# Small steps of a tuned attention-and-SoLU kernel move from VectorE to ScalarE and GpSimd

## The chip, the cores and the metric

The kernel runs on one NeuronCore of a Trainium2 chip. The metric is the device time of one execution in microseconds (us), as the median of several runs. The core's engines run side by side, each through its own list of instructions in order: TensorE (PE, with its weight loads as PEld), VectorE (DVE), ScalarE (ACT), GpSimd (POOL), and SyncE (SP), which issues the DMA transfers. An instruction that waits for another engine holds everything behind it on its own.

## The reference

Set attention with 32 inducing points, then a feed-forward block with the SoLU activation and a layer norm. There are 4 batches of 12608 rows of 128.

```python
def mab(q, kv):
    s = scale * (q @ kv.transpose(0, 2, 1))
    s = s - s.max(-1, keepdims=True)
    a = np.exp(s)
    a /= a.sum(-1, keepdims=True) + 1e-09
    return a @ kv
h = mab(I, x)            # x: (4, 12608, 128), I: (4, 32, 128)
x = mab(x, h)            # then reshaped to (50432, 128)
...
h = x @ w_in             # (50432, 1024)
e = np.exp(h - np.max(h, axis=-1, keepdims=True))
solu = h * (e / (np.sum(e, axis=-1, keepdims=True) + 1e-09))
mu = np.mean(solu, axis=-1, keepdims=True)
var = np.mean((solu - mu) ** 2, axis=-1, keepdims=True)
ln = (solu - mu) / np.sqrt(var + 1e-06) * g_ln
return ln @ w_out        # (50432, 128)
```

## The kernel before

Rows are worked in tiles of 128, 99 tiles a batch (the last one is half full), 396 in all. Tiles of the feed-forward part go in groups of four, and five groups (20 tiles) share one *finish*. There are 20 finishes.

The stages:

- **First pass of a batch** (`p1`): blocks of 12 or 16 tiles are loaded, transposed, scored against the inducing points, and pooled with a running maximum. Batch 0's runs at the start by itself; the first passes of batches 1 to 3 run beside the main work of the batch ahead of them. `P1_STEP` sets how many tiles apart their blocks start.
- **Attention of a block of 16 tiles** (`p2`): scores, transposition (line 840) and maximum (842) on DVE, subtraction on POOL (845), exponential on ACT (852), transposes on PE (875) and copies on ACT (889). The row sums `nr` are reduced on DVE (908), negated with 1e-9 added (911), and inverted to `rn` (914). The negated norm is there so that the next stage's minimum is the negative of a maximum.
- **Main work, tile by tile** (`main`, `soft`): a matmul with the attention's result folded into `w_in` (PE, 1013) leaves 128x1024 in PSUM (`h`). DVE scales it by `rn` into `hn` and takes the minimum `nm` (1054, "the norm"). ACT takes the exponential into `e` with its sum (1065). POOL multiplies `hn` by `e` (1069, "the product"). ACT squares that for the sum of squares (1080), and DVE transposes it in 32x32 blocks into `vt` (1093). The sums go through DRAM to their places (`floor`, 1110 and 1118, by DMA).
- **Second matmul** (`products`, 1136, PE) by `w_out`, with a column of ones that gives each row's total, in two streams. A copy out of PSUM (`evacuate`, 1159) runs on DVE or ACT, whichever the planner has free first.
- **Finish** (`finish`, 1185 to 1198, then 1205): for 20 tiles at once, on 128x20 numbers. Variance from the sum of squares and the total, a floor `z` from the sum of exponentials, the inverse root through `Ln` and `Exp` on ACT, and one Newton step. Then POOL scales the five groups' results by `y` (1205) and SP stores them (1217).

In the program's names, `eu` and `spare` are buffers of 128x1024 that hold `e` or `hn`; `fin` is the finish's small tiles; `dl` is the sums as they come back from DRAM; `qe` is where ACT leaves them.

The order on each engine is made when the program is built. A planner (`Planner.run`) keeps a clock for each engine, a cost for every operation (the second argument of `Op`), and delays between engines; among the operations that could start soon it takes the one with the lowest priority number. The constants `PR_*` are added to the tile's number `t` to make that priority: `PR_MU` the product, `PR_SQ` the square, `PR_TU` the transposition, `PR_G2` the second matmul. `finish` asks for its operations one after the other, each with the operations that it has to wait for; each of DVE's small ones is entered at a cost of 75 ns.

Buffers are handed out by locks. Of the four tiles of `spare` that are free after the start, `HN_MORE` go to the lock for `hn` (which has three others) and the rest to the one for `e` (which has five).

Of the kernel before, what the change touches and what calls it, by code (L numbers as in the profile page):

```python
# [13 lines left out]
AF = mybir.ActivationFunctionType  # L14
ALU = mybir.AluOpType
# [7 lines left out]
FF = 1024  # L23
# [29 lines left out]
EUS = 5  # L53
SPARES = 9
H_LAST = -30
HN_MORE = 3
RAWS = 2
FILL = 400
FIRST = 4
LATE = -15  # L60
P1_FROM = 3
P1_GO = -20
P1_STEP = 11
P2_AHEAD = 35
P2_START = 35
PR_EX = -2
PR_EV = -20
PR_FI = 40
PR_G2 = 4
PR_HN = -4  # L70
PR_MU = 1
PR_SQ = 1
PR_TU = 4
RUSH = -100.0
SLACK = {"PE": 0, "ACT": 200, "DVE": 100, "POOL": 100, "SP": 0}
SPARE = 150
# [53 lines left out]
class Planner:  # L130
# [8 lines left out]
    def spawn(self, gen, prio):  # L139
        self._step([gen, prio, 0], None)  # L140
# [8 lines left out]
    def give(self, lock, buf, *after):  # L149
        lock.free.append((buf, after))  # L150
        while lock.free and lock.waiting:
            lock.waiting.sort(key=lambda w: (w[2], w[1]))
            task = lock.waiting.pop(0)[0]
            self.blocked -= 1
            self._step(task, lock.free.pop(0))
# [95 lines left out]
def set_attention_then_solu_kernel(ctx: ExitStack, tc: tile.TileContext, x, inducing, w_in, w_out, g_ln, out):  # L251
    nc = tc.nc
    NB, N, _ = x.shape
    scale = 1.0 / float(C) ** 0.5
# [26 lines left out]
    def buf(shape, name, dtype=F32, where=None):  # L281
        return (where or const).tile(shape, dtype, name=name)
# [7 lines left out]
    def small(i, **widths):  # L290
# [42 lines left out]
    tiny = buf([P, 1], "tiny")  # L333
# [6 lines left out]
        out=fold[:, 0, :], in_=ident.rearrange("p (q m) -> p m q", m=M), op=ALU.add, axis=AX.X  # L340
    )
    for q in range(1, 4):
# [4 lines left out]
        out=quarter, in_=ident.rearrange("p (q m) -> p q m", m=M), op=ALU.add, axis=AX.X  # L347
# [45 lines left out]
    def dma(nbytes, fn, *after, prio=None, issue=450):  # L393
        return Op("SP", issue + DMA_GAP, fn, *after, prio=prio, moves=nbytes)
# [411 lines left out]
    def p2(b, j):  # L806
        s0, n = at_groups[b][j]
# [3 lines left out]
        for k, (g0, gn) in enumerate(p1_groups[b]):  # L811
            if g0 < s0 + n and s0 < g0 + gn:
                d = yield xd_done[(b, k)]
                prev += d
        xT, rel = yield X2
        d = yield dma(
            n * P * C * 4,
            lambda: nc.sync.dma_start(xT[:, :n, :].rearrange("p s t -> p (s t)"), xT_dram[b][:, s0 * P : (s0 + n) * P]),
            rel, prev,
        )  # L820
# [8 lines left out]
        def scores():  # L829
            for g in range(4):  # L830
# [7 lines left out]
        d = yield Op("PE", SWITCH + n * 60, scores, d, rel, hd)  # L838
        give(X2, xT, d)
        d = yield Op("DVE", 66 + 33.4 * n, lambda: nc.vector.transpose(out=s2[:, :n, :].rearrange("p s m -> p (s m)"), in_=sp[:, : n * M]), d, srel)  # L840
        give(bank, sp, d)
        d = yield Op("DVE", 66 + 33.4 * n, lambda: nc.vector.tensor_reduce(out=mx[:, :n], in_=s2[:, :n, :], op=ALU.max, axis=AX.X), d)  # L842
        d = yield Op(
            "POOL", 60 + 61.4 * n,
            lambda: nc.gpsimd.tensor_tensor(  # L845
                out=s2[:, :n, :], in0=s2[:, :n, :], in1=mx[:, :n].unsqueeze(2).to_broadcast([P, n, M]), op=ALU.subtract
            ),
            d,
        )
        a4, arel = yield A4  # L850
        twice = s2[:, :n, None, :].to_broadcast([P, n, 2, M])
        de = yield Op("ACT", 90 + 54 * n, lambda: nc.scalar.activation(a4[:, :n], twice, AF.Exp, scale=scale), d, arel)
# [53 lines left out]
        for _ in range(2):  # L906
            spawn(turned_rows(), PRIO_P2(b, j))
        d = yield Op("DVE", 66 + 33.4 * n, lambda: nc.vector.tensor_reduce(out=nr[:, :n], in_=a4[:, :n, 0, :], op=ALU.add, axis=AX.X), de)
        d = yield Op(
            "DVE", 75,  # L910
            lambda: nc.vector.tensor_scalar(out=nr[:, :n], in0=nr[:, :n], scalar1=-1.0, scalar2=-1e-9, op0=ALU.mult, op1=ALU.add),  # L911
            d,
        )
        dr = yield Op("DVE", 138, lambda: nc.vector.reciprocal(rn[:, :n], nr[:, :n]), d, rel)
        give(S2, (s2, mx, nr), dr)
        plan.set(turned_too, dr)
# [55 lines left out]
    def PRIO_P1(b, k):  # L972
        return -20.0 + k if b == 0 else NT * (b - 1) + P1_FROM + P1_STEP * k + P1_GO

# [70 lines left out]
    def soft(t, b, j, s, hp, d):  # L1045
# [22 lines left out]
        give(NM, nm, de)  # L1068
        d = yield Op("POOL", 2330, lambda: nc.gpsimd.tensor_tensor(out=e, in0=hn, in1=e, op=ALU.mult), de, prio=t + PR_MU)  # L1069
        give(HN, hn, d)  # L1070
# [7 lines left out]
        def square():  # L1078
            ds = yield Op(
                "ACT", 1040, lambda: nc.scalar.activation(sq, e, AF.Square, scale=1.0 / 32.0, accum_out=G["qe"][:, s, 0:1]), d,  # L1080
                prio=t + PR_SQ,
            )
# [13 lines left out]
            ),  # L1096
            d, rel, prio=t + PR_TU,
        )
# [24 lines left out]
    def products(b, j, t, w):  # L1123
# [21 lines left out]
        ready = max(d.end + AFTER[d.eng]["PE"] for a in (G["turned"], rel, wc_ready.after) for d in a if d is not None)  # L1145
        stream[w].update(j=0, emit=emit, ready=ready, close=close, prio=t + PR_G2)
        idle = flow["idle"]
# [3 lines left out]
    def evacuate(b, j, w, op, bank, dop, prio):  # L1151

        F = fin[(b, j // FG)]
        rows = ff_groups[j][1] * M
        i0 = j % FG * 4 + 2 * w
        rel = yield F["buf"]

        def copied(eng):
            return lambda: eng(F["raw"][:rows, i0 : i0 + 2, :], op[:rows, :, : C + 1])  # L1159

        d = yield Op("DVE", 340, copied(nc.vector.tensor_copy), dop, rel, prio=prio, alt=Op("ACT", 265, copied(nc.scalar.copy), dop, rel, prio=prio))
        give(H, bank, d)
        F["out"].append(d)
        F["left"] -= 1
        if not F["left"]:
            spawn(finish(b, j // FG), prio + PR_FI)

    def finish(b, f):
        F = fin[(b, f)]
        js = [j for j in range(NG) if j // FG == f]  # L1170
        rows = ff_groups[js[0]][1] * M
        w = 4 * len(js)
        fd = []
        for j in js:
            d = yield grp[(b, j)]["floor"]
            fd += d
        part, v, y, root, z = (F[k][:rows, :w] for k in ("part", "v", "y", "root", "z"))
        Q, S = (F["dl"][:rows, :w, i] for i in range(2))
        tt, ts, stt = nc.vector.tensor_tensor, nc.vector.tensor_scalar, nc.vector.scalar_tensor_tensor
        total = F["raw"][:rows, :w, C]  # L1180

        def small(fn, *after):
            return Op("DVE", 75, fn, *after)

        de = yield small(lambda: ts(out=z, in0=S, scalar1=1e-3, scalar2=1e-12, op0=ALU.mult, op1=ALU.add), fd)  # L1185
        de = yield small(lambda: tt(out=z, in0=z, in1=z, op=ALU.mult), de)  # L1186
        d = yield small(lambda: stt(out=part, in0=total, scalar=1.0 / (FF * FF), in1=total, op0=ALU.mult, op1=ALU.mult), F["out"])  # L1187
        d = yield small(lambda: tt(out=v, in0=Q, in1=part, op=ALU.subtract), fd, d)
        d = yield small(lambda: stt(out=v, in0=v, scalar=0.0, in1=z, op0=ALU.max, op1=ALU.add), d, de)

        def inverse():
            nc.scalar.activation(y, v, AF.Ln)
            nc.scalar.activation(root, y, AF.Exp, scale=-0.5)

        da = yield Op("ACT", 330, inverse, d)
        d = yield small(lambda: stt(out=z, in0=root, scalar=-0.5, in1=root, op0=ALU.mult, op1=ALU.mult), da)
        d = yield small(lambda: tt(out=z, in0=z, in1=v, op=ALU.mult), d)  # L1197
        dy = yield small(lambda: stt(out=y, in0=z, scalar=1.5, in1=root, op0=ALU.add, op1=ALU.mult), d, da)
        used = []
        for j in js:  # L1200
            i0 = j % FG * 4
            raw = F["raw"][:rows, i0 : i0 + 4, :C]

            def scaled(eng):
                return lambda: eng.tensor_tensor(out=raw, in0=raw, in1=y[:, i0 : i0 + 4].unsqueeze(2).to_broadcast([rows, 4, C]), op=ALU.mult)  # L1205

            done = yield Op("POOL", 1000, scaled(nc.gpsimd), dy, prio=OS_PRIO)
            spawn(stored(b, f, j, raw, done), 0)
# [34 lines left out]
    for b in range(NB):  # L1243
        if b:
            for k in range(NP[b]):
                starts.setdefault(NT * (b - 1) + int(P1_FROM + P1_STEP * k), []).append((p1(b, k), PRIO_P1(b, k)))
        starts.setdefault(max(0, NT * (b - 1)), []).append((combine(b), PRIO_P1(b, NP[b] - 1) if b else -28))
        for j in range(len(at_groups[b])):
            starts.setdefault(max(0, NT * b + at_groups[b][j][0] - P2_START), []).append((p2(b, j), PRIO_P2(b, j)))

    def handover():
# [20 lines left out]
        for i in range(at, SPARES):  # L1272
            give(HN if i < at + HN_MORE else EU, spare[:, more + i * FF : more + (i + 1) * FF], *done)
        for v in vt_b:
# [48 lines left out]
```

## Time and profile before

| what | value |
|---|---|
| median of 3 runs | 1381.25 us (1380.73 to 1383.75) |
| the profiled execution | 1387.33 us, of which the span 1385.1 us |
| TensorE's mean granted clock over the span | 0.947 of full speed |
| busy: PE, DVE, ACT, POOL | 1236.7, 1255.2, 1062.2, 1072.8 us |

The span goes from the first to the last instruction that the profiler recorded. Busy time counts an engine's own work, without its queue's waits; a busy PE is not PE at its peak, since its matmuls overlap. The page cuts the span into 40 slices and gives each engine's busy share of them in tenths. Slices 1 and 2 hold the start, slices 3 to 31 the batches with a first pass beside them, the others the last batch and the tail:

```profile
PE   9889999989988989899989998689998998989785
DVE  5698899999999899999998999999999899999992
ACT  5588688968877877878887787578787787789681
POOL 2577587959876978878887778678788796889793
PEclk9879899999999999999999999899999999999897
```

Groups of instructions give the line, engine and operation, what is written and read, sizes and count; then busy us, mean ns of one, and the idle time of the engine just before them with what ended it.

### The profile page before, as it was taken

How to read it: one execution, taken by the hardware profiler on the slowest of the kernel's cores; microseconds unless marked ns; L12 is line 12 of the kernel's file. 1: busy time of each engine (PE TensorE's matmuls, PEld its weight loads, DVE VectorE, ACT ScalarE, POOL GpSimd, SP SyncE). 2: the span in 40 equal slices, each digit the busy share in tenths (PEclk: the TensorE clock that was granted, in tenths of full speed). 3: DMA queues.
4: the chain of work that ended last, by engine and by line, in shares of the span. 5: the costliest groups of instructions: out<-in, count | busy, mean ns of one | idle time of the engine just before them, and what ended most of it. 6: DMA issues, size and time to landing. Idle time of an engine off the chain costs nothing. (4 is left out here: it accounts for less than half of the span.)

```text
span 1385.1 us, 77913 instructions
## 1 busy us (share of the span) xinstructions
PE 1236.7 (89%) x35557; PEld 1142.9 (83%) x35557; DVE 1255.2 (91%) x1882; ACT 1062.2 (77%) x2015; POOL 1072.8 (77%) x557
## 2 busy tenths in 40 slices
PE   9889999989988989899989998689998998989785
PEld 7678888978887978888878887688888887889784
DVE  5698899999999899999998999999999899999992
ACT  5588688968877877878887787578787787789681
POOL 2577587959876978878887778678788796889793
PEclk9879899999999999999999999899999999999897
DMA  9552242203231325312213324121222020201102
GB/s 365 187 162 65 82 138 65 85 17 103 60 123 50 100 65 156 87 44 55 82 45 123 117 78 125 47 88 30 67 70 73 4 70 19 63 4 43 31 16 75
DMA packets 152905, 113.58 MB, mean 82 GB/s; under 512 B 76256, under 2 KB 132608, under 8 KB 148096
## 3 DMA queue, kind: packets, MB, share of 16 engines
q1 hardware_dynamic: 152576, 108.62, 26.2%
q8 instruction: 277, 4.54, 1.4%
q14 instruction: 52, 0.43, 0.1%
HBM read 54.30 MB, written 52.18 MB: 77 GB/s over the span
## 5 line engine op out<-in xcount | busy, mean ns | idle before, releaser
L1136 PE MATMUL h<-wc,vt 32*128 32x129 f32 x25600 | 1068.9, 280 | 34.0 <-issue 17.1
L1136 PEld LDWEIGHTS h<-wc,vt 32*128 32x128 f32 x25600 | 1023.8, 191 | 71.3 <-issue 40.5
L1013 PE MATMUL h<-hs,aT 32*128 32x128 f32 x6336 | 459.6, 286 | 81.0 <-DVE spare L1054 46.6
L1069 POOL TENSOR_TENSOR eu<-hn,eu 128x1024 f32<-128x1024 f32 x197 | 463.3, 2372 | 77.4 <-ACT eu L1065 75.5
L1013 PEld LDWEIGHTS h<-hs,aT 32*128 32x128 f32 x6336 | 408.0, 196 | 109.1 <-DVE spare L1054 53.5
L1093 DVE STREAM_TRANSPOSE vt<-eu 128x1024 f32<-128x1024 f32 x330 | 402.6, 1228 | 1.3 <-POOL eu L1069 1.0
L1080 ACT ACTIVATE sq<-eu 128x1024 bf16<-128x1024 f32 x330 | 347.2, 1052 | 31.0 <-POOL eu L1069 25.5
L1069 POOL TENSOR_TENSOR eu<-spare,eu 128x1024 f32<-128x1024 f32 x133 | 313.7, 2375 | 58.8 <-ACT eu L1065 56.0
L1054 DVE TENSOR_SCALAR_CACHE_REDUCE hn<-h,rn 128x1024 f32<-128x1024 f32 x198 | 248.6, 1261 | 29.7 <-PE h L1013 20.5
L1054 DVE TENSOR_SCALAR_CACHE_REDUCE spare<-h,rn 128x1024 f32<-128x1024 f32 x198 | 248.8, 1260 | 25.8 <-PE h L1013 23.2
L1065 ACT ACTIVATE eu<-hn,nm 128x1024 f32<-128x1024 f32 x197 | 224.9, 1143 | 25.4 <-DVE hn L1054 19.6
L1069 POOL TENSOR_TENSOR spare<-spare 128x1024 f32<-128x1024 f32 x65 | 154.2, 2372 | 31.6 <-ACT spare L1065 31.4
L1065 ACT ACTIVATE eu<-spare,nm 128x1024 f32<-128x1024 f32 x133 | 151.9, 1143 | 24.8 <-DVE spare L1054 20.4
L1205 POOL TENSOR_TENSOR spare<-spare,fin 128x512 f32<-128x512 f32 x100 | 101.0, 1042 | 46.7 <-issue 32.1
L1159 ACT COPY spare<-h 128x258 f32<-128x258 f32 (+1 forms) x119 | 43.7, 371 | 112.1 <-PE h L1136 111.6
L1093 DVE STREAM_TRANSPOSE vt<-spare 128x1024 f32<-128x1024 f32 x66 | 80.8, 1225 | 0.3 <-POOL spare L1069 0.2
L1065 ACT ACTIVATE spare<-spare,nm 128x1024 f32<-128x1024 f32 x65 | 74.3, 1143 | 4.1 <-DVE spare L1054 3.7
L1080 ACT ACTIVATE sq<-spare 128x1024 bf16<-128x1024 f32 x66 | 69.3, 1050 | 4.9 <-POOL spare L1069 3.8
L1080 ACT ACTIVATION_READ_ACCUMULATOR sq<-eu 128x1 f32 x330 | 62.7, 190 | 0.0
L1159 DVE COPY spare<-h 128x258 f32<-128x258 f32 (+1 forms) x81 | 32.7, 410 | 33.1 <-PE h L1136 32.7
L583 PE MATMUL h<-ident,xn 32*128 32x32 f32 x1188 | 54.3, 227 | 6.6 <-DVE spare L1054 3.7
L845 POOL TENSOR_TENSOR s<-s,mx 128x512 f32<-128x512 f32 (+3 forms) x29 | 26.7, 922 | 42.4 <-DVE mx L842 41.3
(162 smaller groups left out, 971.5 us busy)
## 6 DMA issues: line engine op xcount, KB each, us to landing
out_dram<-spare SPq DMA_DIRECT2D x96, 256.0 KB, 3.7
xT<-xd SPq DMA_DIRECT2D x19, 1024.0 KB, 5.4
xn<-in_x_dram SPq DMA_DIRECT2D x15, 1024.0 KB, 6.6
xd<-xT SPq DMA_DIRECT2D x15, 1024.0 KB, 4.7
dl<-dd SPq DMA_DIRECT2D x396, 1.0 KB, 2.6
xd<-vt SPq DMA_DIRECT2D x7, 768.0 KB, 10.4
spare<-in_x_dram SPq DMA_DIRECT2D x5, 768.0 KB, 12.5
xT<-xd SPq DMA_DIRECT2D x5, 768.0 KB, 4.4
```

The source lines that it names most:

```text
L583: nc.tensor.transpose(out=tr[:, k * 512 + s * M : k * 512 + (s + 1) * M], in_=xn[r, s, :], identity=ident[r, r])
L845: lambda: nc.gpsimd.tensor_tensor(out=s2[:, :n, :], in0=s2[:, :n, :], in1=mx[:, :n].unsqueeze(2).to_broadcast([P, n, M]), op=ALU.subtract),
L1013: nc.tensor.matmul(hp[:, cols], lhsT=aT[rows, i // 2, :], rhs=hs[rows, cols], start=True, stop=True)
L1054: lambda: nc.vector.tensor_scalar(out=hn, in0=hp, scalar1=rn, scalar2=None, op0=ALU.mult, op1=ALU.min, accum_out=nm),
L1065: "ACT", 1133, lambda: nc.scalar.activation(e, hn, AF.Exp, bias=nm, scale=-1.0, accum_out=G["qe"][:, s, 1:2]), d, rel, srel,
L1069: d = yield Op("POOL", 2330, lambda: nc.gpsimd.tensor_tensor(out=e, in0=hn, in1=e, op=ALU.mult), de, prio=t + PR_MU)
L1080: "ACT", 1040, lambda: nc.scalar.activation(sq, e, AF.Square, scale=1.0 / 32.0, accum_out=G["qe"][:, s, 0:1]), d,
L1093: lambda: nc.vector.transpose(out=G["vtb"][:, : n * FF].rearrange("p (j s t) -> p j s t", j=M, s=n)[:, :, s, :], in_=e.rearrange("p (a f) ...
L1136: nc.tensor.matmul(op[:rows, a - 2 * w, : C + 1], lhsT=vt[q, k, :], rhs=wc[q, k, :], start=(k == 0), stop=(k == JB - 1))
L1159: return lambda: eng(F["raw"][:rows, i0 : i0 + 2, :], op[:rows, :, : C + 1])
L1205: return lambda: eng.tensor_tensor(out=raw, in0=raw, in1=y[:, i0 : i0 + 4].unsqueeze(2).to_broadcast([rows, 4, C]), op=ALU.mult)
```

## The change

The small steps leave DVE. Steps with one input go to ACT as activations (`Square`, `Relu`, `Copy`), products and sums of two tiles to POOL. The negation of `nr` becomes an activation. The planner's constants get other values. Lines behind the change move up by 3 to 7.

```diff
-HN_MORE = 3
+HN_MORE = 4
-P1_STEP = 11
+P1_STEP = 10.5
-PR_G2 = 4
+PR_G2 = 8
-PR_MU = 1
-PR_SQ = 1
-PR_TU = 4
+PR_MU = -4
+PR_SQ = 4
+PR_TU = 12
...
-        d = yield Op(
-            "DVE", 75,
-            lambda: nc.vector.tensor_scalar(out=nr[:, :n], in0=nr[:, :n], scalar1=-1.0, scalar2=-1e-9, op0=ALU.mult, op1=ALU.add),
-            d,
-        )
+        d = yield Op("ACT", 100, lambda: nc.scalar.activation(nr[:, :n], nr[:, :n], AF.Copy, scale=-1.0, bias=-1e-9), d)
...
-        de = yield small(lambda: ts(out=z, in0=S, scalar1=1e-3, scalar2=1e-12, op0=ALU.mult, op1=ALU.add), fd)
-        de = yield small(lambda: tt(out=z, in0=z, in1=z, op=ALU.mult), de)
-        d = yield small(lambda: stt(out=part, in0=total, scalar=1.0 / (FF * FF), in1=total, op0=ALU.mult, op1=ALU.mult), F["out"])
-        d = yield small(lambda: tt(out=v, in0=Q, in1=part, op=ALU.subtract), fd, d)
-        d = yield small(lambda: stt(out=v, in0=v, scalar=0.0, in1=z, op0=ALU.max, op1=ALU.add), d, de)
+        gt, act = nc.gpsimd.tensor_tensor, nc.scalar.activation
+        dz = yield Op("ACT", 135, lambda: act(z, S, AF.Square, scale=1e-3, bias=tiny[:rows]), fd)
+        d = yield Op("ACT", 135, lambda: act(part, total, AF.Square, scale=1.0 / FF), F["out"])
+        d = yield Op("POOL", 205, lambda: gt(out=v, in0=Q, in1=part, op=ALU.subtract), fd, d)
+        d = yield Op("ACT", 135, lambda: act(v, v, AF.Relu), d)
+        d = yield Op("POOL", 205, lambda: gt(out=v, in0=v, in1=z, op=ALU.add), d, dz)
 
         def inverse():
-            nc.scalar.activation(y, v, AF.Ln)
-            nc.scalar.activation(root, y, AF.Exp, scale=-0.5)
-
-        da = yield Op("ACT", 330, inverse, d)
-        d = yield small(lambda: stt(out=z, in0=root, scalar=-0.5, in1=root, op0=ALU.mult, op1=ALU.mult), da)
-        d = yield small(lambda: tt(out=z, in0=z, in1=v, op=ALU.mult), d)
-        dy = yield small(lambda: stt(out=y, in0=z, scalar=1.5, in1=root, op0=ALU.add, op1=ALU.mult), d, da)
+            act(y, v, AF.Ln)
+            act(root, y, AF.Exp, scale=-0.5)
+            act(z, root, AF.Square)
+
+        da = yield Op("ACT", 465, inverse, d)
+        d = yield Op("POOL", 205, lambda: gt(out=z, in0=z, in1=v, op=ALU.mult), da)
+        d = yield Op("ACT", 135, lambda: act(z, z, AF.Copy, scale=-0.5, bias=1.5), d)
+        dy = yield Op("POOL", 205, lambda: gt(out=y, in0=z, in1=root, op=ALU.mult), d)
```

What the built programs show of it: DVE, in the third batch, at the eleventh finish, before the change. `fin` are the finish's tiles, L1093 is a transposition, L1159 an evacuation, L1054 a norm.

```order
L1185 TENSOR_SCALAR fin_109<-dl_108 128x20
L1093 STREAM_TRANSPOSE vt<-eu 128x32x32
L1186 TENSOR_TENSOR fin_109<-fin_109 128x20
L1187 SCALAR_TENSOR_TENSOR fin_109<-spare 128x20
L1159 COPY spare<-h_694 128x258
L1159 COPY spare<-h_697 128x258
L1188 TENSOR_TENSOR fin_109<-dl_108,fin_109 128x20
L1189 SCALAR_TENSOR_TENSOR fin_109<-fin_109 128x20
L1054 TENSOR_SCALAR hn_81,nm_114<-h_696,rn_97 128x1024
```

After the change DVE has none of these steps. The same finish begins on ACT (squares L1177 and L1178, the relu L1180) like this, among squares of tiles (L1076), exponentials (L1061) and the negation of a block of 16 tiles (L909):

```order
L1177 ACTIVATE fin_109<-dl_108,tiny 128x20
L1178 ACTIVATE fin_109<-spare 128x20
L1076 ACTIVATE sq,qe_102<-eu 128x1024 x2
L1180 ACTIVATE fin_109<-fin_109 128x20
L593 COPY xT<-h_695 128x2x16x32
L852 ACTIVATE a_93<-s_0_87 128x1024
L1061 ACTIVATE eu,qe_104<-hn_80,nm_114 128x1024
L909 ACTIVATE nr_89<-nr_89 128x16
```

The relu now waits for POOL, with a copy and exponentials behind it. The same finish ends on POOL like this (the Newton step's products L1189 and L1191, the scaling L1198), between products of tiles (L1065) and an attention block's subtraction (L845):

```order
L845 TENSOR_TENSOR s_1_90<-s_1_90,mx_91 128x512
L1065 TENSOR_TENSOR eu<-spare,eu 128x1024 x3
L1189 TENSOR_TENSOR fin_109<-fin_109 128x20
L1065 TENSOR_TENSOR eu<-hn_82,eu 128x1024
L1191 TENSOR_TENSOR fin_109<-fin_109 128x20
L1198 TENSOR_TENSOR spare<-spare,fin_109 128x4x128 x5
```

Each small step stands between products, where before only the scaling stood. For the negated norm, DVE at the thirteenth block of attention, before:

```order
L908 TENSOR_REDUCE nr_89<-a_93 128x16
L741 SCALAR_TENSOR_TENSOR acc_126<-acc_126,small_121,h_694 128x128
L911 TENSOR_SCALAR nr_89<-nr_89 128x16
L1093 STREAM_TRANSPOSE vt<-eu 128x32x32
L914 RECIPROCAL rn_95<-nr_89 128x16
L1054 TENSOR_SCALAR hn_82,nm_115<-h_696,rn_97 128x1024
```

and after:

```order
L908 TENSOR_REDUCE nr_89<-a_93 128x16
L1089 STREAM_TRANSPOSE vt<-eu 128x32x32
L1155 COPY spare<-h_694 128x258
L910 RECIPROCAL rn_95<-nr_89 128x16
L1089 STREAM_TRANSPOSE vt<-eu 128x32x32
L1050 TENSOR_SCALAR spare,nm_115<-h_697,rn_97 128x1024
```

Between the reduction and the reciprocal a transposition and an evacuation stand in place of the negation, which has gone to ACT.

More of the change, by code (lines that the diff above doesn't have):

```diff
@@ L1178, in finish @@
         Q, S = (F["dl"][:rows, :w, i] for i in range(2))
-        tt, ts, stt = nc.vector.tensor_tensor, nc.vector.tensor_scalar, nc.vector.scalar_tensor_tensor
         total = F["raw"][:rows, :w, C]
[L1182 to L1186, printed above, removed]
-        d = yield small(lambda: stt(out=part, in0=total, scalar=1.0 / (FF * FF), in1=total, op0=ALU.mult, op1=ALU.mult), F["out"])
-        d = yield small(lambda: tt(out=v, in0=Q, in1=part, op=ALU.subtract), fd, d)
-        d = yield small(lambda: stt(out=v, in0=v, scalar=0.0, in1=z, op0=ALU.max, op1=ALU.add), d, de)
-        def inverse():
-            nc.scalar.activation(y, v, AF.Ln)
-            nc.scalar.activation(root, y, AF.Exp, scale=-0.5)
-        da = yield Op("ACT", 330, inverse, d)
-        d = yield small(lambda: stt(out=z, in0=root, scalar=-0.5, in1=root, op0=ALU.mult, op1=ALU.mult), da)
-        d = yield small(lambda: tt(out=z, in0=z, in1=v, op=ALU.mult), d)
-        dy = yield small(lambda: stt(out=y, in0=z, scalar=1.5, in1=root, op0=ALU.add, op1=ALU.mult), d, da)
+        gt, act = nc.gpsimd.tensor_tensor, nc.scalar.activation
[4 more added lines that the diff above has]
+        d = yield Op("POOL", 205, lambda: gt(out=v, in0=v, in1=z, op=ALU.add), d, dz)
+        def inverse():
+            act(y, v, AF.Ln)
[5 more added lines that the diff above has]
+        dy = yield Op("POOL", 205, lambda: gt(out=y, in0=z, in1=root, op=ALU.mult), d)
         used = []
```

## The prediction

> **What bounds the kernel now.** I read the page first: its span and the busy time of each engine.
>
> ```profile
> span 1385.1 us, 77913 instructions
> PE 1236.7 (89%) x35557; PEld 1142.9 (83%) x35557; DVE 1255.2 (91%) x1882; ACT 1062.2 (77%) x2015; POOL 1072.8 (77%) x557
> ```
>
> VectorE (DVE) is the fullest of the engines whose busy time is plain. Next come busy times by stretch: the main stage, from the first norm to the last, and its final quarter, in which no first pass of another batch runs.
>
> ```profile
> 54.00:1341.00 1287.00, 1162.41 (x34239) 1079.72 (x34241) 1203.53 (x1746) 1023.21 (x1922) 1033.35 (x517) 0.95 0.26 73
> 1042.00:1341.00 299.00, 265.76 (x8043) 256.56 (x8041) 285.41 (x370) 236.04 (x451) 253.41 (x127) 0.94 0.16 37
> ```
>
> After the length come PE, PEld, DVE, ACT, POOL. DVE is busy 1203.5 of 1287 us (93.5%), ScalarE (ACT) 79.5%, GpSimd (POOL) 80.3%. What of DVE's time is the work that the change moves? The same view for the instructions that touch the finish's tiles (DVE, ACT, POOL), and for line 911 (DVE):
>
> ```profile
> 0.00:1386.00 1386.00, 120.30 (x160) 8.63 (x40) 101.04 (x100) 0.95 0.28 82
> 0.00:1386.00 1386.00, 55.24 (x29) 0.95 0.28 82
> ```
>
> So 189 instructions on 4 to 20 elements a partition take 175.5 us, 0.93 us each. The spread by line (minimum/median/maximum ns) says why that is odd:
>
> ```profile
> L911 DVE TENSOR_SCALAR nr<-nr x29: 131/1258/9143, 50.7 to 1283.1; 128x16 f32<-128x16 f32 x19, 128x12 f32<-128x12 f32 x5, 128x7 f32<-128x7 f32 x4, 128x4 f32<-128x4 f32 x1
> L1186 DVE TENSOR_TENSOR fin<-fin x20: 127/1201/2334, 156.5 to 1372.9; 128x20 f32<-128x20 f32 x20
> L1189 DVE SCALAR_TENSOR_TENSOR fin<-fin x20: 131/178/2361, 159.1 to 1373.4; 128x20 f32<-128x20 f32 x20
> L1054 DVE TENSOR_SCALAR_CACHE_REDUCE hn<-h,rn x198: 1182/1270/1285, 53.7 to 1339.9; 128x1024 f32<-128x1024 f32 x198
> L1093 DVE STREAM_TRANSPOSE vt<-eu x330: 1178/1233/1245, 68.7 to 1357.5; 128x1024 f32<-128x1024 f32 x165
> ```
>
> The small steps can be done in 0.13 us and take up to 9.1; the big norms and transposes never vary. The timeline at two of the long ones:
>
> ```profile
> 862.99 8.84 DVE L911 TENSOR_SCALAR nr<-nr 128x16 f32<-128x16 f32 x1
> 864.85 6.95 POOL L1069 TENSOR_TENSOR eu<-hn,eu 128x1024 f32<-128x1024 f32 x3
> 871.74 1.27 DVE L1054 TENSOR_SCALAR_CACHE_REDUCE spare<-h,rn 128x1024 f32<-128x1024 f32 x1
> ...
> 1343.95 7.63 DVE L1185 TENSOR_SCALAR fin<-dl 128x20 f32<-128x20 f32 x1
> 1344.53 7.02 POOL L1069 TENSOR_TENSOR eu<-hn,eu 128x1024 f32<-128x1024 f32 x3
> 1354.66 2.75 PE L1136 MATMUL h<-wc,vt 32*128 32x129 f32 x44 [6.22 <-DVE vt L1093]
> ```
>
> The step that starts at 862.99 ends at 871.83; POOL's run of products ends at 871.80. The one at 1343.95 ends at 1351.58, POOL's run at 1351.55. A small step starts, and is held until POOL pauses; DVE can do nothing behind it. At 1354.66 TensorE (PE) has waited 6.22 us for transposes that stood behind such a step. The Trainium skill (SBUF: State Buffer, section "SBUF: two separate sides") says that VectorE and GpSimd share one port pair under an exclusive lock, taken by VectorE operations in a two-port mode or with two SBUF inputs; the ends 0.03 us behind POOL's agree.
>
> **The change, part by part.** *Removed from DVE:* 160 + 29 small steps, 175.5 us. How much lies on the path? The chain of waits, for the stretch that it covers, by line, and line 911, 1185 and 1186 in that stretch:
>
> ```profile
> by line: PE h L1136 31.3%; issue 12.4%; PE h L1013 10.6%; DVE vt L1093 9.5%; DVE hn L1054 6.5%; DVE spare L1054 5.1%; DVE nr L911 3.7%; DVE fin L1185 1.9%; POOL spare L1205 1.9%; POOL eu L1069 1.6%; DVE fin L1186 1.1%; ACT eu L1065 1.1%; DV
> 793.50:1385.10 591.60, 33.74 (x11) 0.94 0.20 54
> 793.50:1385.10 591.60, 18.39 (x10) 0.94 0.20 54
> 793.50:1385.10 591.60, 11.95 (x10) 0.94 0.20 54
> ```
>
> The three lines have 6.7% of 591.6 us on the chain, 39.6 of their 64.1 us: a share of 0.62. Over all small steps that is 0.62 x 175.5 = 109 us, the lower end of the gain.
>
> *Added to ACT and POOL.* The nearest rows: ACT on 128x20, ACT with a pointer as bias, POOL's two-input operation at two sizes and its smallest one; then the evacuation copy, of which the new order gives 8 more to ACT (81 to 73 on DVE).
>
> ```profile
> L1193 ACT ACTIVATE fin<-fin 128x20 f32<-128x20 f32 x20 | 4.4, 219 | 0.6
> L692 ACT ACTIVATE small<-m,small 128x1 f32<-128x1 f32 x26 | 7.6, 291 | 20.0 <-DVE small L684 20.0
> L845 POOL TENSOR_TENSOR s<-s,mx 128x512 f32<-128x512 f32 x19 | 19.9, 1050 | 24.4 <-DVE mx L842 23.4 <-DVE fin L1189 0.9
> L845 POOL TENSOR_TENSOR s<-s,mx 128x128 f32<-128x128 f32 x1 | 0.4, 400 | 0.0
> L703 POOL TENSOR_SCALAR l<-l,small 128x1 f32<-128x1 f32 x12 | 4.6, 380 | 21.9 <-ACT eT L694 11.2 <-ACT wc L694 4.8 <-ACT spare L694 4.2
> L1159 ACT COPY spare<-h 128x258 f32<-128x258 f32 x114 | 41.9, 371 | 97.3 <-PE h L1136 96.8
> ```
>
> ACT gets five steps for each of 20 finishes and 29 negations: 129 x 0.219 = 28 us (20 with a pointer bias at 0.291: 1.4 more), and 8 x 0.371 = 3: 1055 us in the stage. POOL gets four for each finish: 1.69 ns an element between the two L845 rows puts 20 elements at 0.22 us, 80 of them at 17 us; L703 as upper bound makes it 30. I take 17, since it is the same operation: 1051 us. DVE falls to about 1025.
>
> The Trainium skill (ScalarE: Activation LUTs, section "Rules for kernel authors"; GPSIMD Engine Reference, section "4.1 Engine selection") speaks against this: relu, add and mul belong on VectorE, and two-input elementwise work is about twice as slow on GpSimd. For steps that nothing holds up it is borne out mildly (0.18 us on DVE against 0.22, at the tail below); by the rule alone the sum would be 189 x 0.04 = 8 us more than before. The held rows above outweigh it.
>
> With DVE emptied, three engines carry 1025 to 1055 us. If the fullest is filled as DVE is now, the stage takes 1055 / 0.935 = 1128 us: a gain of 159, the upper end. At the lower end, 109, the stage is 1178 and the fill 89.6%. I take the middle, 134, because three full engines in one cycle wait for each other more than one full engine does with two slack ones.
>
> *New handovers.* A finish now crosses POOL and ACT seven times (four into POOL, three into ACT), and each negation goes DVE, ACT, DVE. What today's crossings cost, in all, times, longest:
>
> ```profile
> ACT fin L1192 <- DVE fin L1189: 18.7, 8, 5.5
> POOL spare L1205 <- DVE fin L1198: 14.0, 7, 2.8
> ACT eu L1065 <- DVE vt L1093: 9.6, 4, 5.1
> POOL eu L1069 <- ACT eu L1065: 131.5, 60, 6.6
> ```
>
> Over 20 finishes that is 0.94 and 0.70 us for each. ACT has 69 crossings more (65 us), POOL 60 (42 us); behind a waiting step stand exponentials on ACT and products on POOL. Both fit into the 97 to 101 us that a stage of 1152 us leaves idle there, which is why I don't take the upper end. DVE's reciprocal now waits for ACT with norms behind it: 29 x 0.94 = 27 us at most, nothing at least, since other norms and transposes stand between; taken as nothing, kept for the range.
>
> *The constants.* They reorder, and issue nothing more. One spare tile goes from the exponentials (6 to 5) to the norms (6 to 7). Exponentials that wait for a tile to be transposed away cost 9.6 us now; at worst as much again, inside ACT's idle time, so nothing. No DMA is added or taken away; on SP's queue the same transfers stand in places that differ by a few, and the finish's stores are released by the same GpSimd operation as before.
>
> *The tail.* The last finish stands alone:
>
> ```profile
> 1372.65 0.18 DVE L1185 TENSOR_SCALAR fin<-dl 128x20 f32<-128x20 f32 x1
> 1373.60 0.22 ACT L1192 ACTIVATE fin<-fin 128x20 f32<-128x20 f32 x1 [0.85 <-DVE fin L1189]
> 1374.84 2.04 POOL L1205 TENSOR_TENSOR spare<-spare,fin 128x512 f32<-128x512 f32 x2 [13.25 <-issue]
> ```
>
> From 1372.65 to 1374.84 are 2.2 us; ten steps of 0.22 with seven crossings at some 0.05 (an estimate from these rows) make 2.6: 0.4 us more.
>
> *The sum.* The profiled execution took 1387.3 us, 6.1 over the median of 1381.25, and 2.2 over its span. 1387.3 - 134 + 0.4 = 1253.7, and as a median 1247.6.
>
> Can PE deliver? Two stretches without a small step on DVE, all engines, then line 1054 alone (two instructions a tile):
>
> ```profile
> 252.10:273.30 21.20, 21.20 (x622) 19.43 (x614) 20.26 (x35) 19.37 (x40) 21.14 (x12) 1.00 0.34 100
> 1252.50:1273.70 21.20, 20.32 (x682) 20.03 (x678) 21.09 (x28) 19.36 (x37) 21.20 (x11) 1.00 0.13 26
> 252.10:273.30 21.20, 10.15 (x17) 1.00 0.34 100
> 1252.50:1273.70 21.20, 11.33 (x19) 1.00 0.13 26
> ```
>
> Eight tiles in 21.2 us with another batch's first pass, nine without: 2.65 and 2.36 us a tile, against 1287 / 396 = 3.25 now and 1152 / 396 = 2.91 forecast. PE and POOL keep up where DVE isn't held.
>
> **The rivals.**
> 1. *Something else binds sooner.* PE has 42% of the chain (31.3 + 10.6) and 90% of the stage. If its 1162 us shrink little, or the 27 us at the reciprocals are real, the gain is 82 to 109 us or less: 1275 to 1340, typically 1300. The two stretches speak against it, the chain for it.
> 2. *All of it is on the path and nothing replaces it.* 1387.3 - 175.5 - 6.1 = 1206, and less if the stage fills to the 95.5% of its last quarter. Equal loads on three engines speak against it.
> 3. *Slower: POOL in step with ACT.* POOL idles 254 us of the stage now. If none of that comes from held DVE steps, it stays, and 17 us of work and 42 us of crossings come on top: 1440. It decides where POOL's old waits shrink by less than 59 us. POOL's 21.14 of 21.20 us in the first stretch speaks against it.
> 4. *The hold only moves.* Another DVE instruction is held in place of the small ones, and the moved steps cost 8 us more: 1381 to 1389. Norms and transposes run through POOL's products at an unvarying length, so there is nothing to hold. The two rules quoted above end here.
>
> **How the numbers follow.** Forecast (gain 109 to 170, 1211 to 1272): 0.62. Rival 1: 0.18. Rival 2: 0.12. Rival 3: 0.04. Rival 4: 0.04, shared between no change and slower. The range goes from 1205 (rival 2) to 1300 (the lower end less the reciprocals' 27 us) and leaves out 2 in 10. Faster by over 0.2% (what a measurement can tell here from no change): 0.92; within: 0.02; slower: 0.06.
>
> **What would show it.** After, DVE's busy time near 1080 us with no instruction under 128x32 over 1 us; ACT near 1093 and POOL near 1090; the crossings in the list of waits at about 1 us each. Wrong would be: POOL's small steps far over 0.22 us, POOL's wait for exponentials growing past 131.5 us, or PE's idle time unchanged.

## The result, and the profile after

The changed kernel took 1245.0 us (median of 4 runs, 1242.1 to 1248.7) against 1381.1 us for the kernel before: a ratio of 0.901, with a 95% interval of 0.899 to 0.904. Its profiled execution took 1244.1 us, of which the span 1242.3. The prediction said 1247.6, range 1205 to 1300.

The page of the changed kernel, span and busy times:

```profile
span 1242.3 us, 77962 instructions
PE 1196.1 (96%) x35557; PEld 1112.9 (90%) x35557; DVE 1092.8 (88%) x1684; ACT 1085.6 (87%) x2152; POOL 1087.8 (88%) x638
```

VectorE gave up 162 us of busy time, and TensorE, which was busy for 89% of the span, is so for 96%. TensorE's mean granted clock rose from 0.947 to 0.979 of full speed. Its busy time fell in just that proportion, with the same number of matmuls: 1236.7 x 0.947 is 1171.2, and 1196.1 x 0.979 is 1171.0. Busy times by stretch, for the main stage from its first norm to its last (us from the start; length; PE, PEld, DVE, ACT, POOL):

```profile
54.00:1205.00 1151.00, 1124.02 (x34188) 1051.64 (x34187) 1050.52 (x1567) 1042.07 (x2044) 1042.50 (x588) 0.98 0.29 82
```

The stage went from 1287 to 1151 us. VectorE, ScalarE and GpSimd are now within 9 us of each other, at 91% each, and TensorE is at 98%.

Groups by line and shape for the moved steps (busy us, mean ns, idle time of the engine before them):

```profile
L1177 ACT ACTIVATE fin<-dl,tiny 128x20 f32<-128x20 f32 x20 | 6.0, 302 | 0.0
L1178 ACT ACTIVATE fin<-spare 128x20 f32<-128x20 f32 x20 | 4.5, 224 | 0.0
L909 ACT ACTIVATE nr<-nr 128x16 f32<-128x16 f32 x19 | 3.9, 208 | 2.0 <-DVE nr L908 2.0
L1179 POOL TENSOR_TENSOR fin<-dl,fin 128x20 f32<-128x20 f32 x20 | 4.8, 238 | 1.8 <-ACT fin L1178 1.8
L1191 POOL TENSOR_TENSOR fin<-fin 128x20 f32<-128x20 f32 x20 | 4.5, 227 | 3.3 <-ACT fin L1190 3.3
```

Each takes 0.21 to 0.30 us in the mean. What had cost 0.93 us each on VectorE costs a quarter to a third of that on the other two engines. The list of waits has the new crossings (in all, times, longest):

```profile
POOL fin L1189 <- ACT fin L1186: 10.3, 8, 2.0
POOL fin L1181 <- ACT fin L1180: 8.1, 7, 2.9
POOL fin L1191 <- ACT fin L1190: 3.3, 6, 1.3
POOL fin L1179 <- ACT fin L1178: 1.8, 2, 1.5
ACT nr L909 <- DVE nr L908: 2.0, 4, 0.8
ACT fin L1190 <- POOL fin L1189: 1.2, 3, 0.4
DVE rn L910 <- ACT nr L909: 1.3, 3, 0.7
POOL eu L1065 <- ACT eu L1061: 83.7, 54, 6.3
```

GpSimd waits 23.5 us for them, ScalarE about 4 us, VectorE 1.3. GpSimd's wait for exponentials shrank from 131.5 to 83.7 us, although it has more to do; before, it also waited 37.9 us for exponentials that lay in tiles of `spare`, a wait that is gone. The chain of waits, from 700 us on (it covers the last part of the span, as before):

```profile
by line: POOL eu L1065 31.2%; PE h L1132 27.2%; PE h L1009 6.2%; POOL spare L1198 5.2%; issue 4.4%; ACT sq L1076 3.2%; ACT eu L1061 3.1%; DVE vt L1089 1.9%; DVE spare L1050 0.9%; PE h L725 0.9%; DVE hn L1050 0.8%; PE h L833 0.8%; ACT a L852
```

VectorE, a third of the chain before, has all but left it. TensorE and GpSimd have about a third of it each.

The kernels of the experiments ran in several jobs, each beside fresh runs of the kernel before, which went from 1361 to 1389 us; runs over 1.5% above the fastest of their kernel in a job are left out of the medians and ratios. So ratios are given, and differences of under 10 us are not read as more than a direction.

### The profile page after: what moved, and what is told of

Same layout as the page of the kernel before. It is cut to its first block, busy times and chain, and to the rows that moved or that the text cites. A ratio compares the mean times of both kernels' runs of the same rounds, so it can differ in the third digit from the quotient of the medians.

```text
span 1242.3 us, 77962 instructions
## 1 busy us (share of the span) xinstructions
PE 1196.1 (96%) x35557; PEld 1112.9 (90%) x35557; DVE 1092.8 (88%) x1684; ACT 1085.6 (87%) x2152; POOL 1087.8 (88%) x638
## 5 line engine op out<-in xcount | busy, mean ns | idle before, releaser
L1132 PE MATMUL h<-wc,vt 32*128 32x129 f32 (+1 forms) x25600 | 1030.4, 275 | 22.4 <-issue 13.7
L1132 PEld LDWEIGHTS h<-wc,vt 32*128 32x128 f32 (+1 forms) x25600 | 992.7, 186 | 60.6 <-issue 38.6
L1065 POOL TENSOR_TENSOR eu<-spare,eu 128x1024 f32<-128x1024 f32 x227 | 535.7, 2376 | 45.3 <-ACT eu L1061 45.0
L1089 DVE STREAM_TRANSPOSE vt<-eu 128x1024 f32<-128x1024 f32 x396 | 481.6, 1230 | 13.5 <-POOL eu L1065 12.9
L1076 ACT ACTIVATE sq<-eu 128x1024 bf16<-128x1024 f32 x396 | 416.7, 1052 | 47.5 <-POOL eu L1065 37.0
L1065 POOL TENSOR_TENSOR eu<-hn,eu 128x1024 f32<-128x1024 f32 x169 | 399.7, 2377 | 38.9 <-ACT eu L1061 38.7
L1061 ACT ACTIVATE eu<-spare,nm 128x1024 f32<-128x1024 f32 x227 | 259.1, 1142 | 10.3 <-DVE spare L1050 7.8
L1061 ACT ACTIVATE eu<-hn,nm 128x1024 f32<-128x1024 f32 x169 | 192.9, 1142 | 7.4 <-DVE hn L1050 4.8
L1198 POOL TENSOR_TENSOR spare<-spare,fin 128x512 f32<-128x512 f32 x100 | 101.2, 1044 | 1.4
L1076 ACT ACTIVATION_READ_ACCUMULATOR sq<-eu 128x1 f32 x396 | 74.8, 189 | 0.0
L583 PEld LDWEIGHTS h<-ident,xn 32*128 32x128 f32 x1188 | 50.4, 136 | 0.7 <-issue 0.5
L593 ACT COPY xT<-h 128x1024 f32<-128x1024 f32 (+2 forms) x42 | 37.8, 901 | 10.1 <-PE h L583 9.8
L1061 ACT ACTIVATION_READ_ACCUMULATOR eu<-spare,nm 128x1 f32 x227 | 43.0, 190 | 0.0
```

What stands on the lines that cost most here:

```text
L583: nc.tensor.transpose(out=tr[:, k * 512 + s * M : k * 512 + (s + 1) * M], in_=xn[r, s, :], identity=ident[r, r])
L593: lambda: nc.scalar.copy(xT.rearrange("c s (q t) -> c q s t", q=4)[:, 2 * w : 2 * w + 2, :n, :], tr.rearrange("c (k x) -> c k x", k=2)[:, ...
L1061: "ACT", 1133, lambda: nc.scalar.activation(e, hn, AF.Exp, bias=nm, scale=-1.0, accum_out=G["qe"][:, s, 1:2]), d, rel, srel,
L1089: lambda: nc.vector.transpose(out=G["vtb"][:, : n * FF].rearrange("p (j s t) -> p j s t", j=M, s=n)[:, :, s, :], in_=e.rearrange("p (a f) ...
L1132: nc.tensor.matmul(op[:rows, a - 2 * w, : C + 1], lhsT=vt[q, k, :], rhs=wc[q, k, :], start=(k == 0), stop=(k == JB - 1))
```

## Experiments: the steps or the constants?

The change has two parts. The first two experiments separate them; the next two divide the steps.

**Steps alone.** The changed kernel with the old constants:

```diff
-HN_MORE = 4
+HN_MORE = 3
-P1_STEP = 10.5
+P1_STEP = 11
-PR_G2 = 8 ; PR_MU = -4 ; PR_SQ = 4 ; PR_TU = 12
+PR_G2 = 4 ; PR_MU = 1 ; PR_SQ = 1 ; PR_TU = 4
```

> The new homes of the small steps, with the planner's constants as they were before. Hold theory (a small VectorE step waits for GpSimd's running products to end, and taking these steps away is the gain): at least three quarters of the 136 us come, 1245 to 1280 us. Order theory (the new constants arrange the engines better, the steps matter little): 1330 us or more.

1264.1 us, ratio 0.922 (0.915 to 0.929). The steps alone bring 109 us against the 1373.1 us of the kernel before in that job, or 117 against the first job's 1381.1: the hold theory's range.

**Constants alone.** The same lines, the other way, in the kernel before.

> The new constants alone; the small steps stay on VectorE. Hold theory: the steps are held as before, 1350 to 1400 us, and the 189 steps still take some 175 us. Order theory: 1250 to 1300 us.

1384.1 us, ratio 1.008 (1.002 to 1.013): a little slower. The small steps of this kernel on the finish's tiles (DVE, ACT, POOL) and on line 911 (DVE), in the view by stretch:

```profile
0.00:1450.00 1450.00, 140.53 (x160) 8.57 (x40) 102.12 (x100) 0.95 0.26 78
0.00:1450.00 1450.00, 26.37 (x29) 0.95 0.26 78
```

They take 167 us on VectorE, as the hold theory has it. The order theory falls: the constants bring nothing while the steps are held. Yet with the steps moved, they are worth 1264.1 - 1245.0 = 19 us, and the runs of the two don't overlap (1261.7 to 1268.2 and 1242.1 to 1248.7). The two kernels ran in different jobs; by their ratios, 0.922 and 0.901, it is 28 us.

**The negation alone.** The `nr` step goes to ScalarE as in the change, the rest stays as before.

> Only the 29 negations go to ScalarE; the finish stays on VectorE, constants as before. They took 55 of the 175.5 us. Hold theory: the gain is 0.62 to 1 times 55, so 1326 to 1347 us. Rival, the hold moves: the finish's steps that stay run into GpSimd's products more often and eat it, 1365 us or more, with more than 140 us on the finish's VectorE steps (120 before).

1364.2 us, ratio 0.993 (0.989 to 0.998): 9 us. The expected 34 at least didn't come. The finish's tiles in the same view, and the first of its steps, by line:

```profile
0.00:1450.00 1450.00, 136.56 (x160) 8.61 (x40) 101.48 (x100) 0.96 0.26 78
```

```profile
L1181 DVE TENSOR_SCALAR fin<-dl 128x20 f32<-128x20 f32 x20 | 48.9, 2443 | 0.2
```

The finish's steps went from 120 to 137 us on VectorE; its first one from 1305 to 2443 ns in the mean. So part of the hold moved, as the rival had it, though not all: VectorE's small steps shrank by 39 us and the time by 9. The traces show where the rise comes from: five of the 20 steps at L1181 outlasted two to four GpSimd instructions that had started after them, and took 35.8 us together; before, two outlasted one and three, with 12.2 us. Why more of them were passed over in this way was not tried by itself.

**The finish alone.** The finish's steps move as in the change, line 911 stays on VectorE, old constants.

> Only the finish's steps go to ScalarE and GpSimd; the negation stays on VectorE, constants as before. They took 120 of the 175.5 us. Hold theory: 0.62 to 1 times 120, so 1261 to 1307 us. If the seven crossings of a finish cost on the path what they cost at worst (2.2 us each into GpSimd), 1350 us or more. The gains of this kernel and of the one with the negation alone should add up to that of both within 20 us.

1297.4 us, ratio 0.945 (0.935 to 0.954): 76 us, inside the range. Line 911 still takes 36.87 us there. The two parts add up to 85 us against 109 together, 24 apart and so a little outside what I had allowed: taking all steps off seems worth more than the sum of taking some off, though the intervals of the three ratios (6, 13 and 10 us either way) leave the size open.

## Experiments: is it the hold?

**The negation in another form, where it was.** The kernel before, each engine's order unchanged; the new form leaves out the added 1e-9, since its second operation makes the sum:

```diff
-lambda: nc.vector.tensor_scalar(out=nr[:, :n], in0=nr[:, :n], scalar1=-1.0, scalar2=-1e-9, op0=ALU.mult, op1=ALU.add),
+lambda: nc.vector.tensor_scalar(out=nr[:, :n], in0=nr[:, :n], scalar1=-1.0, scalar2=None, op0=ALU.mult, op1=ALU.add, accum_out=junk),
```

> The kernel before, its order untouched; the 29 negations stay on VectorE but are written in the form that also sums its result along the row (the sum is thrown away; the 1e-9 is left out). Form theory (what is held is the plain two-number form between SBUF tiles, not every small step): 29 x 0.3 = 9 us of busy time in place of 55, no instance over 0.5 us, and 1330 to 1352 us. Rival (any small VectorE step between SBUF tiles is held): durations up to several us, and 1375 to 1390 us.

1359.1 us, ratio 0.986 (0.980 to 0.992). Line 911 by instruction (minimum/median/maximum ns):

```profile
L911 DVE TENSOR_SCALAR_CACHE_REDUCE nr<-nr x29: 120/129/166, 51.0 to 1254.2; 128x16 f32<-128x16 f32 x19, 128x12 f32<-128x12 f32 x5, 128x7 f32<-128x7 f32 x4, 128x4 f32<-128x4 f32 x1
L911 DVE DVE_READ_ACCUMULATOR nr<-nr x29: 76/83/86, 51.1 to 1254.3; 128x1 f32 x29
```

On the same engine, at the same place, on the same tiles, the step never takes more than 0.17 us, where the plain form took up to 9.1. So the form is held, not the smallness. That the second constant makes the difference is unlikely: line 772, a plain step with one factor and no sum, is held too (four times, 0.31 to 1.72 us for 128x128 in the kernel before, each ending 0.08 us behind a GpSimd instruction). The time fell by 21 us, less than the 29 expected at least; as with the negation alone, the finish's steps took more (138.08 us). The Trainium skill (VectorE: DVE Perf Modes, sections "Mode 2×_2P — use both read ports for one tensor" and "The perf-mode tier table") says that plain `tensor_scalar` on fp32 in SBUF uses both read ports, and gives `tensor_reduce` its 1× mode alone. The row reduction (line 908) was indeed never held before (0.69 us at most for 128x512); the ports themselves no run here shows.

**More held steps.** The changed kernel, its order unchanged, with a step behind each reciprocal whose result nobody reads (the tile `extra` is set up elsewhere):

```diff
-        dr = yield Op("DVE", 138, lambda: nc.vector.reciprocal(rn[:, :n], nr[:, :n]), d, rel)
+        def inverted():
+            nc.vector.reciprocal(rn[:, :n], nr[:, :n])
+            nc.vector.tensor_scalar(out=extra[:, :n], in0=nr[:, :n], scalar1=-1.0, scalar2=-1e-9, op0=ALU.mult, op1=ALU.add)
+        dr = yield Op("DVE", 138, inverted, d, rel)
```

> The changed kernel, its order untouched, with 29 more VectorE steps of the held form behind the reciprocals, into a tile that nobody reads. Hold theory: they take 1 to 2 us each in the mean, 30 to 60 us of VectorE, with ends just behind those of GpSimd's products, and the time grows by 0.62 to 1 times that: 1265 to 1300 us. Rival (VectorE now has room, 12% of the span): within 8 us of the changed kernel.

1294.6 us, 50 more than the changed kernel and 46 more than the next experiment's, which ran in the same job. The group of the extra steps, and one of them in the timeline with GpSimd's products beside it:

```profile
L912 DVE TENSOR_SCALAR extra<-nr 128x16 f32<-128x16 f32 (+3 forms) x29 | 55.9, 1929 | 0.0
```

```profile
351.09 7.23 DVE L912 TENSOR_SCALAR extra<-nr 128x16 f32<-128x16 f32 x1
351.35 4.65 POOL L1069 TENSOR_TENSOR eu<-hn,eu 128x1024 f32<-128x1024 f32 x2
355.96 2.33 POOL L1069 TENSOR_TENSOR eu<-spare,eu 128x1024 f32<-128x1024 f32 x1
358.24 1.27 DVE L1054 TENSOR_SCALAR_CACHE_REDUCE spare<-h,rn 128x1024 f32<-128x1024 f32 x1
```

The step runs from 351.09 to 358.32, GpSimd's three products to 358.29. 56 us of held steps cost 46 to 50 us, though VectorE had 12% of the span free: its idle time doesn't absorb a hold of several us.

**More steps that nothing holds.** The same, with the extra step in the summing form.

> The same 29 extra steps in the form that sums along the row, which nothing should hold: 9 us of VectorE and 1240 to 1256 us. If an extra small step costs by its presence in the queue and not by the hold, as much as the held form.

1248.3 us, 3 more than the changed kernel, as expected. Presence in the queue costs next to nothing:

```profile
L912 DVE TENSOR_SCALAR_CACHE_REDUCE extra<-nr x29: 104/111/126, 51.5 to 1162.7; 128x16 f32<-128x16 f32 x19, 128x12 f32<-128x12 f32 x5, 128x7 f32<-128x7 f32 x4, 128x4 f32<-128x4 f32 x1
```

Together the three settle the mechanism: the same 29 small steps cost VectorE 56 us in the form that waits for GpSimd and about 6 in the one that doesn't, and the time follows. That it is GpSimd that holds them shows in the ends of all long steps, not of two alone: in the kernel before 83 of the 189 steps took over 0.4 us, and each of the 83 ended 0.025 to 0.056 us behind the end of a GpSimd instruction; so did all 22 such steps of the 29 above.

The granted clock goes the same way. It is 0.963 to 0.970 in the four runs with the held extra steps and 0.974 to 0.977 in the four with the summing ones, and the two kernels differ in nothing else. So the lower clock comes with the holds. How much of the 136 us goes through TensorE's clock (0.947 before, 0.979 after) no run shows.

## Experiments: what binds now?

Each takes work off one engine of the changed kernel, the order unchanged.

**Less on GpSimd.** The scaling works on one column of 128 (`raw[:, :, :1]`).

> The changed kernel, its order untouched; the finish's scaling on GpSimd works on one column of 128, which takes about 80 us off GpSimd's busy time (the other columns are stored unscaled). If GpSimd is what binds now (it has the largest share of the chain): 1165 to 1205 us. If TensorE binds (96% busy): 1230 us or more. If three engines bind together: 1205 to 1230.

**Less on ScalarE.** The square works on `e[:, :776]`.

> The changed kernel, its order untouched; ScalarE's squares work on 776 of 1024 columns (the sum of squares leaves out the rest), about 80 us off ScalarE's busy time, spread over all tiles. Taking 80 us off GpSimd gave 5 us. If ScalarE binds: 1170 to 1210 us. If TensorE binds: 1235 us or more.

Busy times of the two, in this order:

```profile
PE 1194.7 (96%) x35557; PEld 1112.3 (90%) x35557; DVE 1090.0 (88%) x1684; ACT 1083.0 (87%) x2152; POOL 1004.8 (81%) x638
```

```profile
PE 1190.2 (96%) x35557; PEld 1110.9 (90%) x35557; DVE 1089.9 (88%) x1684; ACT 1011.1 (82%) x2152; POOL 1086.8 (88%) x638
```

83 us less on GpSimd gave 1240.0 us, 75 us less on ScalarE 1240.6: 5 and 4 us. So the fill of neither engine sets the time by itself. But the scaling had 5.2% of the chain and the squares 3.2%; GpSimd's products, which had 31.2%, were not shortened, and what they are worth stays open.

**Fewer columns on TensorE.** The second matmul leaves out 12 of its 129 columns (it takes `wc[q, k, 12:]`).

> The changed kernel, its order untouched; the second matmul leaves out 12 of 129 output columns (they are stored as they lie in PSUM), which takes some 80 us of matmul off TensorE. If TensorE binds now (96% busy, and GpSimd's 80 us gave only 5): 1165 to 1215 us. If TensorE's busy time is stretched by waits for its inputs, and not the bound: 1230 us or more.

1251.5 us, nothing gained; but the experiment didn't take away what it meant to:

```profile
L1132 PE MATMUL h<-wc,vt 32*128 32x117 f32 (+1 forms) x25600 | 1035.6, 276 | 23.7 <-issue 16.0 <-DVE vt L1089 2.3 <-ACT aT L889 1.9
```

The 25600 matmuls keep TensorE busy for 1035.6 us with 117 columns, and for 1030.4 with 129 in the changed kernel. This one decides nothing.

**Fewer matmuls.** The second matmul leaves out 3 of 32 accumulation steps, weight loads and all:

```diff
         def emit(a, k):
+            if k % 11 == 5:
+                return
```

> The changed kernel, its order untouched; the second matmul leaves out 3 of its 32 accumulation steps, weights and all (9.4% of its instructions, about 95 us of TensorE's busy time by the row for line 1132; the result lacks those steps). Fewer columns did not shorten a matmul (275 ns before and after), so this takes the work away for real. If TensorE binds: 1150 to 1200 us. If no engine binds alone and each waits for the others: 1215 to 1240 us. If TensorE is stretched by its inputs: 1240 us or more.

1225.9 us, 19 less than the changed kernel. TensorE's busy time:

```profile
PE 1163.5 (95%) x33157; PEld 1066.9 (87%) x33157; DVE 1090.1 (89%) x1684; ACT 1083.6 (88%) x2152; POOL 1087.4 (89%) x638
```

It fell by 33 us, not by 95, and the time by 19, 0.6 of that, and to the middle forecast: of the pieces of work tried, TensorE's is worth most now, without being a bound by itself. In the other kernels, all with the same matmul count, busy time times granted clock stays between 1165 and 1184 us, from a span of 1237 us to one of 1385; so most of that time does not depend on how long TensorE had to wait for others. Why leaving out 9% of the second matmul's steps took only 33 us off stays open.

**The tile back.** The changed kernel with `HN_MORE = 3`.

> The changed kernel with the spare tile back where it was (HN_MORE 3: six tiles for the exponentials, six for the norms); the other constants new. With all constants old it took 1264 us, with all new 1245. If the tile is worth nothing, as the prediction has it: 1242 to 1249 us. If the tile is what the constants bring: 1258 to 1268 us. In between, the priorities and the tile share it.

1256.2 us (6 runs, 1246.4 to 1261.2), ratio 0.911 (0.907 to 0.915) against 0.901 for the change. So the spare tile, moved from the exponentials to the norms, brings about 11 of the constants' 19 us (14 of 28 by the ratios); the rest is the priorities' and the start times', which weren't tried apart. VectorE's norms wait for tiles that products free, here first and in the changed kernel behind it:

```profile
DVE hn L1050 <- POOL eu L1065: 14.9, 7, 3.9
DVE spare L1050 <- POOL spare L1065: 3.5, 2, 3.3
DVE spare L1050 <- POOL eu L1065: 2.8, 2, 2.2
```

```profile
DVE hn L1050 <- POOL eu L1065: 6.5, 3, 3.2
DVE spare L1050 <- POOL eu L1065: 5.9, 4, 3.0
```

With the tile back such waits sum to 21.2 us, in the changed kernel to 12.4. The difference of 9 us is about the size of what the tile brings. That these waits lie on the path is not shown.

## Why the prediction was right, and where it was not

- **The mechanism** was right: small steps of one form are held by GpSimd's products, and VectorE's queue with them. The form, the extra steps and the ends 0.03 us behind GpSimd's show it. One reading was too strong: a held step need not wait "until POOL pauses". In the kernel before, 78 of the 83 long steps ended with the GpSimd instruction that was running when they started, and at 45 of all 83 ends the next one followed without a gap; only five, the two shown in the prediction among them, outlasted one to three instructions that had started after them.
- **The share on the path** of 0.62, read from the chain, was the step that carried it: 109 us were worked out, and the steps alone brought 109 (117 against the first job). That the two meet so closely is in part luck. The share is not the same for every step: of the time that VectorE's small steps lost, 0.2 came off the kernel's time with the negation alone, 0.5 with the finish alone and 0.6 with the other form, and 0.8 to 0.9 of the added holds came on top.
- **The constants** were priced at nothing, and brought 19 us (28 by the ratios). This term of the sum was mis-sized. It made up for the next:
- **The upper end** assumed that the fullest of VectorE, ScalarE and GpSimd sets the time, at the fill that VectorE had. Taking 83 us off GpSimd gave 5, and 75 off ScalarE gave 4, so the fill of neither does. The middle between a right lower end and this upper end, 134 us, hit 136 (143 between the two profiled executions) because the constants lay in between; that is luck, and not the reason that the prediction gave for the middle. With the steps' own gain and no price for the constants the forecast would have been about 1272, still inside the range.
- **Added work**: ScalarE's new steps 29 us (forecast 28 to 29), GpSimd's 18.5 (17), in the stage 1042 and 1043 us of busy time (1055 and 1051). VectorE kept 1050 in place of 1025, for two reasons. Of the 175.5 us of small steps only 165.2 lie in the stage from which they were subtracted. And their ends overlap with the next instruction's start, so leaving them out of the trace before frees 146 us of that stage, less than they add up to.
- **The crossings**: 42 us of waits at GpSimd were 23.5, and 65 at ScalarE only 4; "about 1 us each" was too much for both (0.3 us for each of 80 crossings into GpSimd, 0.05 for each of 89 into ScalarE). The price came from a wait for VectorE's held steps (18.7 us for 20 crossings), which went away with them. The same holds for the reciprocals: 27 us at most was 1.3.
- **Rival 1** was half right: TensorE at 98% of the stage has the largest worth of what was tried, and 42% of the chain before had said so. But it let the gain through: TensorE's busy time in the stage shrank by 38 us, as its clock rose, and its idle time from 125 to 27. The prediction had no term for the clock. **Rival 3** fell: GpSimd's idle time in the stage went from 254 to 108 us; most of it went with the steps (over the whole span, from 312 us before to 177 with the steps alone). **Rival 4**, the hold that moves, doesn't fit the whole change but shows when only one part is made: with only the negation moved, the finish's steps rose by 16 us.
- **The tail**: the last finish after the change (0.4 us more was forecast):

```profile
1228.96 0.31 ACT L1177 ACTIVATE fin<-dl,tiny 128x20 f32<-128x20 f32 x1
1231.71 0.23 POOL L1191 TENSOR_TENSOR fin<-fin 128x20 f32<-128x20 f32 x1 [0.33 <-ACT fin L1190]
1232.01 5.03 POOL L1198 TENSOR_TENSOR spare<-spare,fin 128x512 f32<-128x512 f32 x5
```

3.05 us from its first step to the scaling against 2.19: 0.9 more. The steps take 0.22 to 0.31 us there, against 0.18 on VectorE: where nothing is held, VectorE was the faster place.

## What to carry to other kernels

Look at the spread of an instruction's durations, not only at its mean: a tiny step whose minimum is 0.13 us and whose maximum is 9 waits for something inside its own duration, where no list of waits shows it. Price it by its share on the chain, and look for a form or an engine that isn't held before a faster one; and constants tuned around a stall are priced again when the stall goes: here they were worth nothing before and 19 us or more after.

## What was not expected of the hardware

- The same VectorE operation on the same tiles is held in its plain form (up to 9143 ns) and not in the form that also sums its row (166 ns at most, with a median of 83 ns for reading the sum).
- A hold can outlast several GpSimd instructions: the 7.23 us step above waited through three products that all started after it, one behind the other without a pause. Most long steps don't (5 of 83 did in the kernel before, 5 of 22 with the extra steps), and what decides it is not shown.
- With 32-row weights loaded for each matmul, 12 columns fewer of 129 took nothing off the matmuls' busy time (1035.6 us, against 1030.4 with all).
